# Last expert's second layer in the last chunk: one PSUM bank per output block, each block added and stored whole

## The chip, the cores and the metric

The kernel runs on 1 core of one Trainium2 chip. The metric is device microseconds of one execution. The core's engines are named as the profile names them: PE (TensorE, matmuls; PEld is its weight load), DVE (VectorE), ACT (ScalarE), POOL (GpSimd) and SP (SyncE, which only issues DMAs here). A "q" behind an engine's name (SPq, ACTq) means its instruction queue. A store is started by an issue on the queue of SP, ACT or POOL; the data is then moved by 16 DMA engines that all queues share.

## What is computed

The reference is pooled attention, and then a mixture of four experts whose weights are the tokens' normalized domain probabilities:

```python
k_p = k.reshape(B, H, Sp, pool, D).mean(axis=3); v_p = likewise      # B=8 H=8 S=576 D=64, pool 8
attn = softmax(q @ k_p^T / sqrt(D));  x = (attn @ v_p) as 4608 x 512
p = domain_probs / (domain_probs.sum(-1) + 1e-9)
for e in range(4):
    h = maximum(x @ w1[e], 0)          # 512 -> 1024
    out += p[:, e:e+1] * (h @ w2[e])   # 1024 -> 512
```

The output is 4608 x 512 in float32, 8 batches of 576 rows.

## The kernel before, in words

The work goes in nine chunks of 512 tokens. Chunks 0 to 7 are the first 512 rows of each batch; chunk 8, the last, gathers the remaining 64 rows of all eight batches. In chunk 8 a block r (0 to 3) of 128 tokens holds the 64 rows of batch 2r on partitions 0 to 63 and the 64 rows of batch 2r+1 on partitions 64 to 127. The running sum of the experts is `acc` in SBUF: 128 partitions x 4 blocks x 512 columns of float32.

The order of all instructions on every engine is written out by hand (`manual_schedule`, L1069). For each (chunk, expert) the first layer is seven block products on each of two units (`up_product`, L728 for its matmuls), and the second layer of the pair before runs between them as seven products of another kind (`down`, L796), with two PSUM banks called `chains`. The results of `down` go to `acc` in `add` (L875 on DVE, and for one step ACT's L808 and POOL's L810). With the last expert of a chunk, `down` also stores two blocks x 256 columns at a time (L885, SP's queue).

The last pair, chunk 8 and expert 3, has no first layer to run beside, so its second layer is a plain product, `down_last` (matmuls at L855). It runs after everything else on PE. The output falls into 8 pieces, 4 blocks x 2 halves of 256 columns; each piece is 8 matmuls with a free size of 256. The pieces go in the order (block 2, col 0), (3, 0), (2, 1), (3, 1), (0, 0), (1, 0), (0, 1), (1, 1). Two pieces share one PSUM bank of 512 columns, with the exception of the last two, of which the last has `chains[0]`. When both pieces of a pair are done, DVE adds them to `acc` (L875), and `store` (L890) writes the pair: one DMA for each of the two batches, 64 partitions each, on the queues of SP and ACT (for the pair of blocks 0 and 1 in column half 0, SP and POOL). The last two pieces are added and stored singly, again with one DMA per batch. In all there are 10 stores: 5 by SP, 4 by ACT and 1 by POOL.

In these stores the pattern on the DRAM side is arranged with the row as its slowest index, and this is the line that does it:

```python
by_batch = out.rearrange("(b s) d -> s b d", s=S)[NT:S]
```

The columns 256 to 511 of the first half of w2's rows come from `room`, reloaded by `load_last_weights`, as the kernel had overwritten them with weight sums.

Of the kernel before, what the change touches and what calls it, by code (L numbers as in the profile page):

```python
# [17 lines left out]
def kernel(  # L18
# [10 lines left out]
    nc = tc.nc  # L29

    B, H, S, D = q.shape
    E, DM, F = moe_w1.shape
    P = nc.NUM_PARTITIONS
# [3 lines left out]
    NT = 512  # L37
    NR = NT // P
    REM = S - NT
    KC = DM // P  # L40
    FCH = F // P
# [15 lines left out]
    HF, HN, HD, HK = FCH // 2, NT // 2, DM // 2, KC // 2  # L57
    FH = F // 2
    LO, HI = slice(0, HF), slice(HF, FCH)
    BLOCKS = 2  # L60
# [4 lines left out]
    att = psum.tile([P, 2, NT], F32, name="att")  # L65
    units = [None, None]
    chains = [psum.tile([P, NT], F32, name=f"o_ps{i}") for i in range(2)]
# [9 lines left out]
    acc = const.tile([P, NR, DM], F32, name="acc")  # L77
# [701 lines left out]
    def down(c, e, step, flip=0, pooled=()):  # L779
# [34 lines left out]
        if e == E - 1 and step in (1, 4, 5, 6):  # L814
            store(c, row, cols)
# [21 lines left out]
    def last_weights(fc, col):  # L837
        if col and fc < HF:
            return room[:, fc, :]
        return w2_bf[:, E - 1, fc, col * HD:(col + 1) * HD]  # L840

    def down_last(c, e):

        H_sb = hidden[(c, e)]
        banks = units[0] + units[1]
        for row in (1, 0):
            for col in range(2):
                cols = slice(col * HD, (col + 1) * HD)
                both = [banks[2 * row + col]] * BLOCKS
                if not row and col:  # L850
                    both[1] = chains[0]
                ps = [ps[:, j * HD:(j + 1) * HD] for j, ps in enumerate(both)]
                for j in range(BLOCKS):
                    for fc in range(FCH):
                        nc.tensor.matmul(  # L855
                            ps[j], lhsT=H_sb[:, fc // HF, row, fc % HF, j * P:(j + 1) * P],
                            rhs=last_weights(fc, col),
                            start=(fc == 0 and (j == 0 or both[1] is not both[0])),
                            stop=(fc == FCH - 1), skip_group_check=True,
                        )  # L860
                for j in range(BLOCKS):
                    add(ps[j], c, e, row * BLOCKS + j, cols, False)
                    if not row and col:
                        store(c, row, cols, j)
                if row or not col:
                    store(c, row, cols)

    def add(o_ps, c, e, r, cols, first):

        prob = p_all[:, c * NR + r, e:e + 1]  # L870
        dst = acc[:, r, cols]
        if e == 0 and first:
            nc.scalar.activation(out=dst, in_=o_ps, func=ACT.Copy, scale=prob)  # L873
        else:
            nc.vector.scalar_tensor_tensor(  # L875
                out=dst, in0=o_ps, scalar=prob, in1=dst, op0=ALU.mult, op1=ALU.add,
            )

    def store(c, row, cols, j=None):
        rs = slice(row * BLOCKS, (row + 1) * BLOCKS)  # L880
        if j is not None:
            rs = slice(rs.start + j, rs.start + j + 1)
        if c < B:
            rows = out[c * S:c * S + NT, :].rearrange("(p r) d -> p r d", r=NR)
            nc.sync.dma_start(out=rows[:, rs, cols], in_=acc[:, rs, cols])  # L885
        else:
            by_batch = out.rearrange("(b s) d -> s b d", s=S)[NT:S]
            second = nc.scalar if row or cols.start else nc.gpsimd
            for bb, queue in enumerate((nc.sync, second)):
                queue.dma_start(  # L890
                    out=by_batch[:, 2 * rs.start + bb:2 * rs.stop:2, cols],
                    in_=acc[bb * REM:(bb + 1) * REM, rs, cols],
                )

    nc.vector.memset(zeros, 0.0)

# [170 lines left out]
    with tc.manual_schedule(  # L1069
# [39 lines left out]
        for g in range(7 * N + 1):  # L1109
            t, i = divmod(g, 7)  # L1110
# [22 lines left out]
            if g == 7 * (N - 2):  # L1133
                load_last_weights()
        down_last(*order[-1])
# [1 line left out]
_INS = ['q', 'k', 'v', 'moe_domain_probs', 'moe_w1', 'moe_w2']  # L1137
# [26 lines left out]
```

## Time and profile before

| | |
|---|---|
| runs | 490.93 us median of 3 (490.93, 501.43, 489.06) |
| profiled execution's own time | 489.22 us |
| its span, first to last instruction | 487.5 us |
| granted TensorE clock | 1.000 |
| PE busy | 479.6 us (98% of the span) |
| DVE / ACT / POOL busy | 376.7 / 303.8 / 125.2 us |
| `down_last` on PE (L855) | 64 matmuls, from 476.2 us on |
| its last add on DVE | starts at 483.37 us, 0.48 us |

Times inside the execution are counted from the span's start. The profile lists busy time by engine, the chain of work that ended last, groups of instructions with their mean duration, and for DMAs the packets by queue, with the time that packets took as a share of 16 engines over the window asked for. A "packet" of a store is one contiguous run of bytes (here 1 KB, 256 columns of float32); packets of 4 bytes are listed too, among those "under 512 B". "To landing" is the time from a DMA's issue until its semaphore tells of its end.

### The profile page before, as it was taken

How to read it: one execution, taken by the hardware profiler on the slowest of the kernel's cores; microseconds unless marked ns; L12 is line 12 of the kernel's file. 1: busy time of each engine (PE TensorE's matmuls, PEld its weight loads, DVE VectorE, ACT ScalarE, POOL GpSimd, SP SyncE). 2: the span in 40 equal slices, each digit the busy share in tenths (PEclk: the TensorE clock that was granted, in tenths of full speed). 3: DMA queues.
4: the chain of work that ended last, by engine and by line, in shares of the span. 5: the costliest groups of instructions: out<-in, count | busy, mean ns of one | idle time of the engine just before them, and what ended most of it. 6: DMA issues, size and time to landing. Idle time of an engine off the chain costs nothing.

```text
span 487.5 us, 11523 instructions
## 1 busy us (share of the span) xinstructions
PE 479.6 (98%) x4667; PEld 409.1 (84%) x4672; DVE 376.7 (77%) x759; ACT 303.8 (62%) x577; POOL 125.2 (26%) x135
## 2 busy tenths in 40 slices
PE   8999999999999999999999999999999999999996
PEld 4678478898888888888889888888888888888885
DVE  5869799899768976797579866997678766876674
ACT  5778446855676567656765667656755567556650
POOL 8420504254623154016321442111011101010001
PEclk9999999999999999999999999999999999999999
DMA  9999999884897589646954396312111010004003
GB/s 198 204 207 203 206 158 172 95 98 50 107 104 59 87 79 138 41 88 54 157 49 91 28 171 60 69 23 67 34 23 23 23 65 3 12 23 87 1 2 87
DMA packets 104213, 41.97 MB, mean 86 GB/s; under 512 B 74288, under 2 KB 104112, under 8 KB 104160
## 3 DMA queue, kind: packets, MB, share of 16 engines
q0 software_dynamic: 59168, 22.54, 42.7%
q1 hardware_dynamic: 44016, 17.78, 17.3%
q10 hardware_dynamic: 976, 0.92, 0.6%
q8 instruction: 36, 0.59, 0.5%
q14 instruction: 17, 0.14, 0.1%
HBM read 45.69 MB, written 9.44 MB: 113 GB/s over the span
## 4 chain that ended last, share of the span: by engine, by line
PE 88%; DMA 8%; POOL 2%; DVE 1%; issue 0%; POOLq 0%
PE unit L728 41%; PE o_ps L796 40%; DMA wt_bf<-in_v_dram 4%; DMA w_bf<-in_moe_w_dram 3%; PE att L493 2%; PE o_ps L822 1%; PE unit L855 1%; POOL w_bf L207 1%; POOL wt_bf L142 1%; PE att L419 1%; PE unit L419 0%; DVE wt_bf L294 0%; PE att L822 0%; PE att L546 0%; PE att L529 0%
## 5 line engine op out<-in xcount | busy, mean ns | idle before, releaser
L875 DVE SCALAR_TENSOR_TENSOR acc<-o_ps,p_all,acc 128x256 f32<-128x256 f32 (+1 forms) x284 | 126.3, 485 | 50.4 <-PE o_ps L796 34.0
L796 PEld LDWEIGHTS <-H 128*128 128x128 bf16 x1320 | 129.1, 98 | 15.0
L728 PEld LDWEIGHTS <-w_bf 128*128 128x128 bf16 x1088 | 105.2, 98 | 13.0 <-issue 0.2
L708 DVE CUSTOM_DVE_ANT_0 H<-unit,partial 128x512 bf16<-128x512 f32 x128 | 87.4, 685 | 23.8 <-ACT partial L743 11.5
L796 PE MATMUL o_ps<-w_bf,H 128*128 128x256 bf16 x792 | 102.6, 272 | 0.0
L728 PE MATMUL unit<-xT,w_bf 128*128 128x256 bf16 x704 | 100.4, 273 | 0.0
L810 POOL TENSOR_TENSOR acc<-acc,addend 128x512 f32<-128x512 f32 x24 | 30.4, 1266 | 249.0 <-ACT addend L808 189.0
L743 ACT COPY partial<-unit 128x512 f32<-128x512 f32 x128 | 72.2, 591 | 30.0 <-PE unit L728 30.0
L728 PEld LDWEIGHTS <-wu_bf 128*128 128x128 bf16 x816 | 77.6, 98 | 11.7 <-issue 2.5
L728 PE MATMUL unit<-xs,wu_bf 128*128 128x256 bf16 x512 | 77.0, 273 | 0.0
L796 PE MATMUL o_ps<-wt_bf,H 128*128 128x256 bf16 x528 | 68.4, 273 | 0.0
L745 ACT ACTIVATE H<-unit 128x512 bf16<-128x512 f32 x66 | 39.9, 606 | 31.0 <-PE unit L728 30.9
L796 PEld LDWEIGHTS <-S 128*128 128x128 bf16 x528 | 51.7, 98 | 6.0
L749 ACT ACTIVATE H<-unit 128x512 bf16<-128x512 f32 x66 | 39.6, 601 | 25.6 <-PE unit L728 25.3
L741 ACT COPY unit<-unit 128x512 f32<-128x512 f32 x68 | 39.4, 582 | 23.6 <-PE unit L728 18.0
L728 PE MATMUL unit<-xs,w_bf 128*128 128x256 bf16 x256 | 38.4, 273 | 0.0
L873 ACT ACTIVATE acc<-o_ps,p_all 128x256 f32<-128x256 f32 x72 | 30.6, 484 | 9.5 <-PE o_ps L796 7.9
L152 POOL DMA_DIRECT2D kraw<-in_k_dram x20 | 26.5, 1326 | 37.0 <-DMA kraw<-in_k_dram 37.0
L728 PE MATMUL unit<-xT,wu_bf 128*128 128x256 bf16 x240 | 35.7, 272 | 0.0
L796 PE MATMUL o_ps<-wt_bf,S 128*128 128x256 bf16 x264 | 34.2, 273 | 0.0
L796 PE MATMUL o_ps<-w_bf,S 128*128 128x256 bf16 x264 | 34.2, 273 | 0.0
L152 POOL DMA_DIRECT2D vraw<-in_v_dram x20 | 29.0, 1450 | 19.5 <-DMA vraw<-in_v_dram 19.3
(171 smaller groups left out, 509.7 us busy)
## 6 DMA issues: line engine op xcount, KB each, us to landing
out_dram<-acc SPq DMA_DIRECT2D x32, 256.0 KB, 4.3
w_bf<-in_moe_w_dram POOLq DMA_DIRECT2D x12, 512.0 KB, 18.5
q_sb<-in_q_dram POOLq DMA_DIRECT2D x7, 512.0 KB, 11.1
vraw<-in_v_dram POOLq DMA_DIRECT2D x22, 144.0 KB, 6.5
kraw<-in_k_dram POOLq DMA_DIRECT2D x21, 144.0 KB, 6.0
w_bf<-in_moe_w_dram POOLq DMA_DIRECT2D x4, 256.0 KB, 7.1
w_bf<-in_moe_w_dram POOLq DMA_DIRECT2D x1, 1024.0 KB, 13.9
wt_bf<-in_k_dram POOLq DMA_DIRECT2D x4, 144.0 KB, 5.5
```

The lines of the kernel that those rows point to most:

```text
L152: nc.gpsimd.dma_start(out=raw[:], in_=rows_of(src, b, 2 * part, 2 * part + 2), accum_op=ALU.add if part else ALU.bypass)
L493: nc.tensor.matmul(c_ps[:, h // NPAIR, at:at + D + 1], lhsT=expT[:, h, r // 2, r % 2, :], rhs=vp[:, h, :], skip_group_check=True,)
L708: nc.vector._custom_dve(TENSOR_ADD_SAT, out=dst, in0=ps, in1=part, s0=LARGEST, s1=0.0)
L728: nc.tensor.matmul(ps[:, n * HN:(n + 1) * HN], lhsT=lhs[:, kc, f:f + P], rhs=rhs[:, kc, :], start=(not grows and n == 0 and kc == 0), stop ...
L741: nc.scalar.copy(out=banks[1][:], in_=ps)
L743: nc.scalar.copy(out=part[:, step - 2], in_=ps)
L745: nc.scalar.activation(out=quarter(0, 0), in_=ps, func=ACT.Relu)
L749: nc.scalar.activation(out=quarter(0, 1), in_=ps, func=ACT.Relu)
L796: nc.tensor.matmul(ps[:, j], lhsT=lhs[:, i, j * P:(j + 1) * P], rhs=rhs[:, i, :], start=(not grows and i == 0 and j == 0), stop=(i == HF - 1),
L810: nc.gpsimd.tensor_add(out=dst, in0=dst, in1=addend[:])
L873: nc.scalar.activation(out=dst, in_=o_ps, func=ACT.Copy, scale=prob)
L875: nc.vector.scalar_tensor_tensor(out=dst, in0=o_ps, scalar=prob, in1=dst, op0=ALU.mult, op1=ALU.add,)
```

## The change

`down_last` gets a PSUM bank per piece (seven banks in turn, the eighth piece takes the first again), adds each piece as soon as it is done, and stores each piece whole, 128 partitions in one DMA, by SP and ACT in turn. The last piece is stored by both queues, one batch each. The order of the pieces and of their matmuls stays. The store of the other chunks (L885) stays as it is. The pattern on the DRAM side of the new stores is arranged with the batch as its slowest index.

```diff
     def down_last(c, e):
         H_sb = hidden[(c, e)]
-        banks = units[0] + units[1]
-        for row in (1, 0):
-            for col in range(2):
-                cols = slice(col * HD, (col + 1) * HD)
-                both = [banks[2 * row + col]] * BLOCKS
-                if not row and col:
-                    both[1] = chains[0]
-                ps = [ps[:, j * HD:(j + 1) * HD] for j, ps in enumerate(both)]
-                for j in range(BLOCKS):
-                    for fc in range(FCH):
-                        nc.tensor.matmul(
-                            ps[j], lhsT=H_sb[:, fc // HF, row, fc % HF, j * P:(j + 1) * P],
-                            rhs=last_weights(fc, col),
-                            start=(fc == 0 and (j == 0 or both[1] is not both[0])),
-                            stop=(fc == FCH - 1), skip_group_check=True,
-                        )
-                for j in range(BLOCKS):
-                    add(ps[j], c, e, row * BLOCKS + j, cols, False)
-                    if not row and col:
-                        store(c, row, cols, j)
-                if row or not col:
-                    store(c, row, cols)
+        banks = [att[:, 0]] + [unit[bank][:] for bank in range(2) for unit in units] + [chain[:] for chain in chains]
+        blocks = [(r, col) for rows in ((2, 3), (0, 1)) for col in range(2) for r in rows]
+        for n, (r, col) in enumerate(blocks):
+            ps = banks[n % len(banks)][:, 0:HD]
+            cols = slice(col * HD, (col + 1) * HD)
+            for fc in range(FCH):
+                nc.tensor.matmul(
+                    ps, lhsT=H_sb[:, fc // HF, r // 2, fc % HF, (r % 2) * P:(r % 2 + 1) * P],
+                    rhs=last_weights(fc, col),
+                    start=(fc == 0), stop=(fc == FCH - 1), skip_group_check=True,
+                )
+            add(ps, c, e, r, cols, False)
+            store_block(r, cols, (nc.scalar, nc.sync) if n == len(blocks) - 1 else (nc.sync, nc.scalar)[n % 2:][:1])
...
+    def store_block(r, cols, queues):
+        by_batch = out.rearrange("(b s) d -> b s d", s=S)[:, NT:S]
+        n = 2 // len(queues)
+        for i, queue in enumerate(queues):
+            queue.dma_start(
+                out=by_batch[2 * r + i * n:2 * r + (i + 1) * n, :, cols],
+                in_=acc[i * n * REM:(i + 1) * n * REM, r, cols],
+            )
```

`store` loses its branch for the last chunk and its argument j.

More of the change, by code (lines that the diff above doesn't have):

```diff
@@ L877, in add, with store @@
             )
-    def store(c, row, cols, j=None):
+    def store(c, row, cols):
         rs = slice(row * BLOCKS, (row + 1) * BLOCKS)
[L881 to L893, printed above, removed]
+        rows = out[c * S:c * S + NT, :].rearrange("(p r) d -> p r d", r=NR)
+        nc.sync.dma_start(out=rows[:, rs, cols], in_=acc[:, rs, cols])
+    def store_block(r, cols, queues):
[6 more added lines that the diff above has]
+            )
     nc.vector.memset(zeros, 0.0)
```

## The prediction

> **What bounds the kernel now.** I read the page first (span, busy time, chain), then the timeline from 462 us on, then SP's waits, then the DMA view of the tail and of one store in a quiet stretch.
>
> ```profile
> span 487.5 us, 11523 instructions
> PE 479.6 (98%) x4667; PEld 409.1 (84%) x4672; DVE 376.7 (77%) x759; ACT 303.8 (62%) x577; POOL 125.2 (26%) x135
> PE 88%; DMA 8%; POOL 2%; DVE 1%; issue 0%; POOLq 0%
> ```
>
> PE is the bound until its last matmul. The change touches only what starts at 476.2 us, so the question is what that last stretch becomes. The timeline:
>
> ```profile
> 476.07 6.98 PEld L855 LDWEIGHTS <-H 128*128 128x128 bf16 x64
> ...
> 476.46 0.87 DVE L875 SCALAR_TENSOR_TENSOR acc<-o_ps,p_all,acc 128x256 f32<-128x256 f32 x2
> ...
> 478.18 0.88 DVE L875 SCALAR_TENSOR_TENSOR acc<-unit,p_all,acc 128x256 f32<-128x256 f32 x2 [0.86 <-PE unit L855]
> ...
> 479.09 5.58 SPq L890 DMA_DIRECT2D out_dram<-acc  x5
> 479.09 5.30 ACTq L890 DMA_DIRECT2D out_dram<-acc  x4
> ...
> 483.37 0.48 DVE L875 SCALAR_TENSOR_TENSOR acc<-o_ps,p_all,acc 128x256 f32<-128x256 f32 x1 [0.39 <-PE o_ps L855]
> ```
>
> DVE waits for PE before each pair, and the last add ends at 483.85. The last two stores are issued at 483.88, and the span ends at 487.5: 3.6 us are the last store's way and the program's end. SP's queue waits there for the stores:
>
> ```profile
> SPq L1159 <- DMA out_dram<-acc: 1.3, 2, 1.0
> ```
>
> The DMA view of 478 to 487.5 us gives all stores of the tail:
>
> ```profile
> DMA packets 1089, 1.06 MB, mean 111 GB/s; under 512 B 160, under 2 KB 1056, under 8 KB 1088
> ...
> q1 hardware_dynamic: 592, 0.52, 24.3%
> q10 hardware_dynamic: 448, 0.39, 12.7%
> q0 software_dynamic: 48, 0.13, 4.7%
> ```
>
> And the same view of 331 to 333.5 us shows one earlier store (L885, 128 partitions of two 1 KB runs) with nothing beside it; SP issues it at 331.28:
>
> ```profile
> DMA  0000000000000000002599999999997400000000
> ...
> DMA packets 272, 0.26 MB, mean 105 GB/s; under 512 B 16, under 2 KB 272, under 8 KB 272
> ...
> q1 hardware_dynamic: 272, 0.26, 30.8%
> ```
>
> Two readings carry the forecast. First, each hardware store leaves 16 small packets beside its data, however much data it has: 272 = 256 + 16 for L885; 592 = 512 + 5 x 16 for SP's five stores (q1) and 448 = 384 + 4 x 16 for ACT's four (q10). I read them as one mark for each of the 16 DMA engines that took a share. Second, the time of one 1 KB packet on one engine. Quiet: 30.8% of 16 x 2.5 us is 12.3 us, over 256 packets 48 ns. In the tail, where three queues meet: q1 24.3% of 16 x 9.5 us is 36.9 us over 512, 72 ns; q10 19.3 us over 384, 50 ns.
>
> **The change part by part.** *Matmuls.* 64 before and after, the same operands in the same order, 0.109 us apart. Cost 0 as long as no bank is late. The new banks: att's last reader in the trace is at 416.5 (L456); the four unit banks are read last by ACT's L749 at 474.20 (0.60) and DVE's L708 at 475.86 (0.68), the chains by L875 until 477.33. Piece n starts at 476.2 + 0.87 n, so the latest unit bank (piece 4, at 479.7) has 3.2 us in hand, the chains (pieces 5 and 6, at 480.5 and 481.4) 3 us and more; piece 7 takes att again, whose add ends near 477.8. PE ends as before. If a bank were late, its delay would go straight to the end.
>
> *Adds.* Eight of 0.44 to 0.48 us, as before, each now behind its own 0.87 us of matmuls; they keep up with PE. The last one waits for the last matmul in both kernels: 0. The first add moves forward by 0.87: piece 0 is done at 477.31, DVE is free at 477.33, the add ends at 477.8 and the first store is issued at about 477.83 instead of 479.09.
>
> *Issues.* 10 become 9, and POOL's goes (its landing took 3.1 us, off the path). SP issues pieces 0, 2, 4, 6 and half of 7, ACT pieces 1, 3, 5 and half of 7. One issue takes 0.50 to 0.79 us on its queue, and each queue has one in 1.75 us, so SP's for piece 6 (from 483.0) is over by 483.8, just before the last add ends. ACT has no compute after 474.8 and nothing is queued behind its issues; on SP only the program's end is. If an issue took 0.9 us instead, the last would slip 0.05. Cost 0.
>
> *The store's shape.* This is the large unknown. The pairs were written with the row as the slowest index on the DRAM side (64 rows), out of 64 partitions. A whole piece is written with the batch as the slowest index: 2 batches x 64 rows, out of 128 partitions. No store in the trace has a slowest count other than 64 or 128, so its spread over the engines must be bounded. *Lower end:* it goes over 16 engines like all others, 128 packets in 8 x 48 ns = 0.4 us; pieces come every 0.87 us and no queue builds. It may even gain: the last stores landed 2.5 to 2.9 us after issue, the quiet one (by the same view) after 2.1. So -0.6 to 0. *Upper end:* the engines get equal whole slices of the slowest index, as the count of 16 allows in every store shown (4 of 64 rows or 8 of 128 each). Then the only slices that both sides share are two, and 14 of 16 engines stand idle: 64 packets on each of two engines for every piece, 64 x 48 ns = 3.1 us, with a new one each 0.87 us, on the same two engines whichever queue issued it.
>
> I take the upper end: all the stores shown are explained by one cut along the slowest index, and reaching 16 engines from 2 x 64 rows would need a second cut, for which I see no row. The last piece, by two stores of 64 rows each, would still go over 16 engines, but its packets on those two wait behind the rest.
>
> The Trainium skill (DMA: Bandwidth & Descriptors, section "Why a DMA increments its semaphore by 16 and not by 1") states that the engine count is the largest number up to 16 that divides both patterns' slowest counts above 1; by it the pieces have 2 engines and the sum is the one below, where the 16 engines of every store shown would leave it at or a little under the time before. No run here yet shows a store with a small slowest count. The same page ("Rules for kernel authors") speaks for the change in advising one 128-partition transfer over two halves; the trace's 48 ns against 50 and 72 fits that, and by it alone the sum would be some tenths of a us lower.
>
> *The sum.* First issue 477.83; first packet 1.4 later (the tail's first data stands at 480.5 for an issue at 479.09; the quiet store took 0.85): 479.2. Seven pieces x 64 packets, and 2 x 4 of the last stores, are 456 packets on each of the two engines, x 48 ns = 21.9: data ends at 501.1. From the last data to the span's end is 1.4 before (486.1 to 487.5): 502.5. Around the span lie 489.22 - 487.5 = 1.72: **504.2 us**, 15.0 or 3.1% above the profiled execution before. That one lies below the median shown (490.93); on the median the same step gives 505.9. I took 48 ns since the new stores, like the quiet one, have 128 partitions, and since no more than two engines ask for anything. With the 72 ns of the crowded tail the packets take 32.8 and the time is 515.1; with the quicker first packet (0.85) it is 503.7.
>
> **The rivals.** *All 16 engines, not slower.* For it: every store shown. Against it: none of those has the new shape. Then the tail is issued at 483.88 as before, with less ahead of it: 488.6 to 489.3, about 489.0. The point from which this decides: k engines take 128/k x 48 ns for a piece, and keep up with 0.87 us if k is 8 or 16. *Four engines,* if the cut goes one level deeper: 7 x 32 + 8 = 232 packets, 11.1 us, 493.4, still within 2%. *Two engines at the crowded price:* 515.1; for it the 72 ns of q1, against it that 16 engines worked then. *A PE wait for a bank* in place of the pair's shared bank: the 3 us in hand speak against it; a whole missed add costs 0.5 us, 489.7.
>
> **How the numbers follow.** Two engines 0.76 (of this 48 ns likelier than 72), 16 engines 0.19 with the bank wait in it, four or eight 0.05. The likeliest case's own range is 503 to 515. As it holds under 0.8, the range must reach the 16-engine case: 488.6 to 515.1. 2%, about what a measurement of this kernel can tell from no change, is 499.0 on the profiled time and 500.7 on the median; all of the two-engine case lies above both but for a small part: slower 0.75. The rest is within 2%: 0.24. Faster by 2% would need 10 us out of a tail of 3.6: 0.01.
>
> **What would show it.** In the profile after: PE's last matmul and DVE's last add near 483.4 and 483.9 as before (matmul and add steps); first store issued near 477.8; in the tail's DMA view, under 512 B, 2 small packets for each whole store and 16 for each of the last two (7 x 2 + 2 x 16 = 46) if two engines work, 9 x 16 = 144 if all do; a mean DMA share near 2/16 until about 501 us, at some 43 GB/s (2 x 1 KB in 48 ns). A landing that grows from store to store, and an end that waits for it on SP. Wrong would be: 144 small packets and a span near 487; a PE gap at L855; or two engines with a packet well off 48 ns.

## The result, and the profile after

| | before | changed kernel |
|---|---|---|
| median of 6 runs each | 489.07 us (488.51 to 501.43) | 502.50 us (502.01 to 505.64) |
| ratio to before | | 1.0281, 95% interval 1.025 to 1.0312 |
| span of the profiled execution | 487.5 us | 503.9 us |

The change made the kernel slower by 13.4 us (the prediction: 15.0, to 504.2). The ratios in this document leave out executions well above the others of their kernel: the 501.43 us here, and 509.4 us (granted clock 0.942) of the version with four whole stores further below, whose time is given without it. The page after:

```profile
span 503.9 us, 11527 instructions
PE 481.9 (96%) x4672; PEld 410.1 (81%) x4672; DVE 376.7 (75%) x759; ACT 303.7 (60%) x577; POOL 124.7 (25%) x134
PE 93%; ACT 1%; DMA 1%; POOL 1%; issue 0%; DVE 0%; POOLq 0%
```

The span grew by 16.4 us, and PE is busy no more than 2.3 us longer. Three of the 16.4 belong to this one execution and lie far from the change: the granted clock fell between 15 and 20 us, where it was 1.00 before, and all that follows comes 3.0 us later. The other executions of the changed kernel have spans of 500.3 to 501.9 us. The window table of the changed kernel (length, busy time by engine, then PEclk, DMA share, GB/s) has it in its third column from the right:

```profile
15.00:20.00 5.00, 4.61 (x33) 3.65 (x32) 2.05 (x5) 2.04 (x4) 2.75 (x4) 0.50 1.38 204
```

The tail, from the timeline after. Take 3.0 us off each time to lay it beside the one before:

```profile
480.25 0.48 DVE L866 SCALAR_TENSOR_TENSOR acc<-att,p_all,acc 128x256 f32<-128x256 f32 x1
480.76 13.96 SPq L880 DMA_DIRECT2D out_dram<-acc  x5
...
481.69 11.48 ACTq L880 DMA_DIRECT2D out_dram<-acc  x4
...
486.36 0.48 DVE L866 SCALAR_TENSOR_TENSOR acc<-att,p_all,acc 128x256 f32<-128x256 f32 x1 [0.39 <-PE att L851]
```

PE and DVE do what they did: the last add starts at 486.36 - 3.0 = 483.36 (483.37 before), and the first store is issued at 480.76 - 3.0 = 477.8 (479.09 before). But the issues of the two queues stretch over 14.0 and 11.5 us instead of 5.6 and 5.3, and the program's end comes 17 us after the last add instead of 3.6. At the end SP waits for stores, for longer than the 1.3 us of before:

```profile
SPq L1147 <- DMA out_dram<-acc: 7.7, 4, 3.7
```

The DMA view of 470 to 504 us shows why:

```profile
DMA  0000000000000011111111111111423111111100
GB/s 0 0 0 0 19 0 0 0 0 10 0 0 0 0 30 42 29 48 43 45 48 36 48 48 48 48 48 48 116 67 96 48 48 48 48 48 48 48 16 0
DMA packets 1073, 1.08 MB, mean 32 GB/s; under 512 B 46, under 2 KB 1070, under 8 KB 1070
...
q1 hardware_dynamic: 600, 0.59, 5.5%
q10 hardware_dynamic: 470, 0.46, 4.3%
```

A share of one tenth of 16 engines over 20 us, a plateau of 48 GB/s, and 46 small packets. 46 is 7 x 2 + 2 x 16: two engines for each whole store, 16 for each of the last two, which are the short rise between 494 and 496 us.

### The profile page after: what moved, and what is told of

It is laid out like the page before. It is cut to its first block, busy times and chain, and to the rows that moved or that the text cites. A ratio compares the mean times of both kernels' runs of the same rounds, so it can differ in the third digit from the quotient of the medians.

```text
span 503.9 us, 11527 instructions
## 1 busy us (share of the span) xinstructions
PE 481.9 (96%) x4672; PEld 410.1 (81%) x4672; DVE 376.7 (75%) x759; ACT 303.7 (60%) x577; POOL 124.7 (25%) x134
## 4 chain that ended last, share of the span: by engine, by line
PE 93%; ACT 1%; DMA 1%; POOL 1%; issue 0%; DVE 0%; POOLq 0%
PE unit L728 41%; PE o_ps L796 40%; PE o_ps L822 2%; PE att L493 1%; DMA wt_bf<-in_v_dram 1%; PE o_ps L650 1%; PE att L419 1%; POOL wt_bf L142 1%; PE unit L851 1%; PE unit L650 1%; PE o_ps L664 1%; PE unit L419 1%; PE att L664 1%; ACT qT L404 0%; PE att L851 0%; PE o_ps L851 0%
```

## The experiments

The theory under test: a store's engines are set by the slowest count that both sides share (the runs vary it on the DRAM side alone; the SBUF side has 64 or 128 partitions throughout); seven stores with a slowest count of 2 run on two DMA engines, which then have 456 packets of 1 KB each to move. The rivals: the bank per block and the early adds cost the time; a whole block in one DMA blocks its queue, whatever its pattern; only a store near the end costs. Ratios below are to the kernel before on the same chip, with their 95% intervals.

**Each half of the change alone.** First the stores alone, in the kernel before (`store_block` is that of the change):

```diff
+                single = not row and col    # the last two blocks
                 for j in range(BLOCKS):
                     add(ps[j], c, e, row * BLOCKS + j, cols, False)
-                    if not row and col:
-                        store(c, row, cols, j)
-                if row or not col:
-                    store(c, row, cols)
+                    if single:
+                        store_block(row * BLOCKS + j, cols, (nc.scalar, nc.sync) if j else (nc.sync,))
+                if not single:
+                    for j in range(BLOCKS):
+                        store_block(row * BLOCKS + j, cols, ((nc.sync, nc.scalar)[j],))
```

> The kernel before with its shared banks and its paired adds kept; only its stores are replaced by the change's: each block whole, batch slowest on the DRAM side, SP and ACT in turn, the last block by both queues. Theory (two slices of the slowest DRAM index, so two DMA engines carry the seven whole stores): the whole loss, and as the first store is issued about 1.3 us later than with single adds, slightly more: 503 to 504.5 us against about 489 before, 46 small packets. Rival (the loss comes from the bank per block and the early adds): about 489. Rival (a queue that blocks in its issue whatever the pattern): also about 503, so this run does not tell that one apart.

Measured: 504.1 us, ratio 1.0296 (1.0272 to 1.032), 46 small packets. The stores are the whole loss. The time is 1.6 us above the changed kernel's 502.5, as a first store made late by adds in pairs would give, but the two ratios' intervals overlap, so these 1.6 us are not shown.

Then banks and adds alone, in the changed kernel (`store` is that of the kernel before):

```diff
             add(ps, c, e, r, cols, False)
-            store_block(r, cols, ...)
+            row, j = divmod(r, BLOCKS)
+            if not row and col:
+                store(c, row, cols, j)
+            elif j:
+                store(c, row, cols)
```

> The changed kernel's bank per block and single adds, with the stores of the kernel before (pairs, one DMA per batch, row slowest). Theory: no loss, 488.5 to 489.5 us, first store near 479.1 as before, under 512 B 160 packets. Rival (banks and early adds cost the time): about 502. If the bank per block gains something, it is at most 0.5 us.

Measured: 488.44 us, ratio 0.9977 (0.9964 to 0.999), 160 small packets. The rival of the banks is out.

**The same store with another order of indices.** The seven whole stores keep their size, packets, queues and times; what changes is which DRAM index is slowest, and with it the row that each packet goes to:

```diff
+        if len(queues) == 1:
+            by_row = out.rearrange("(b s) d -> s b d", s=S)[NT:S]
+            queues[0].dma_start(out=by_row[:, 2 * r:2 * r + 2, cols], in_=acc[:, r, cols])
+            return
...
```

> The changed kernel with one thing different: the seven whole stores are written with the row as the slowest DRAM index and the batch inside it. Same 128 KB, same 128 one-KB packets, same queue and order, one DMA each. The rows of the last chunk come out permuted in these seven blocks (partition p goes to batch p mod 2, row p div 2), so the output is not the reference's. Theory: all 16 engines again, 144 small packets (9 x 16), 488 to 489.5 us. Rival (a whole store of 128 partitions blocks its queue, or one DMA per block is too much for one queue): 500 us or more, with issues of several us as in the changed kernel.

Measured: 488.57 us, ratio 0.9977 (0.9962 to 0.9992). Its DMA view of 478 to 489.5 us:

```profile
DMA packets 1169, 1.06 MB, mean 92 GB/s; under 512 B 144, under 2 KB 1168, under 8 KB 1168
...
out_dram<-acc SPq DMA_DIRECT2D x4, 128.0 KB, 2.1
out_dram<-acc ACTq DMA_DIRECT2D x3, 128.0 KB, 2.1
```

144 is 9 x 16, and a whole store lands in 2.1 us. A whole block by one queue is no burden that shows; the order of the DRAM indices is worth the 13.9 us between this run and the changed kernel.

**Every block by one DMA per batch,** as the change does with its last:

```diff
-            store_block(r, cols, (nc.scalar, nc.sync) if n == len(blocks) - 1 else (nc.sync, nc.scalar)[n % 2:][:1])
+            store_block(r, cols, (nc.scalar, nc.sync) if n % 2 else (nc.sync, nc.scalar))
```

> The changed kernel with every block stored by both queues, one batch each (64 rows, 64 partitions), as the change does with its last block alone: 16 stores instead of 9. Theory: 16 engines each, 256 small packets, 488 to 489.5 us; against the kernel before possibly 0.3 to 0.8 us less, since the stores start 1.3 us earlier and POOL's store is gone from the tail. Rival (single adds or many issues cost): 490 or more; each queue then has one issue of 0.5 to 0.8 us in 0.87 us, so a late last issue would show at 484 or later on the timeline of before.

Measured: 488.49 us, ratio 0.9981 (0.9965 to 0.9996), 256 small packets. 16 issues cost nothing that shows. Unlike the run with the row slowest, this version puts every row in its place, so it is the repair that a kernel can use.

**Other counts.** With 4 and with 8 as the slowest count, the rows of a batch walked as 4 x 16 and 8 x 8, by batch on both queues:

```diff
...
+            dst = by_batch[2 * r + i, :, cols]
+            if n > 1:    # 4, or 8; 1 for the last block
+                dst = dst.rearrange("(t h) d -> h t d", h=n)
+            queue.dma_start(out=dst, in_=acc[i * REM:(i + 1) * REM, r, cols])
```

> The changed kernel with seven blocks stored by one DMA per batch on both queues, and on the DRAM side 64 rows walked as 4 x 16 (slowest index 4: row 4t + h, h slowest), so the rows inside each batch come out permuted and the output is not the reference's there; the last block as in the change. Theory (the slowest count sets the number of engines): 4 engines, 14 stores x 16 + 8 = 232 packets on each, 224 fewer than in the changed kernel, x 45 ns = 10.1 us less: about 492.4, between 491.5 and 493.5, 14 x 4 + 2 x 16 = 88 small packets. Rival (only a batch as slowest index, or only 2, does it; otherwise a second cut spreads it over 16): 488 to 489.5.

> As the kernel with four slices, with 8 x 8 rows instead (slowest index 8; rows inside a batch permuted, last block as in the change). Theory: 8 engines, 14 x 8 + 8 = 120 packets on each, 5.4 us of work in the 7 us between first and last store, so no backlog: 488 to 489.5 us, 14 x 8 + 2 x 16 = 144 small packets. This is the point at which the prediction said that the engines keep up. Rival (any small slowest count costs in proportion): 490 or more.

Measured: 493.76 us with four (ratio 1.0095, 1.0065 to 1.0125), 489.15 us with eight (ratio 1.0008, 0.9989 to 1.0026). The DMA views, first of the kernel with four over 476 to 491.7 us:

```profile
GB/s 0 0 0 0 0 5 42 86 73 97 81 65 50 50 63 37 55 81 78 97 89 97 86 76 83 97 99 99 120 164 162 180 102 94 94 84 10 0 0 0
DMA packets 1113, 1.06 MB, mean 67 GB/s; under 512 B 88, under 2 KB 1112, under 8 KB 1112
```

and of the kernel with eight over 476 to 487.3 us:

```profile
DMA packets 1169, 1.06 MB, mean 94 GB/s; under 512 B 144, under 2 KB 1168, under 8 KB 1168
```

Both counts of small packets are as expected (14 x 4 + 2 x 16 = 88; 14 x 8 + 2 x 16 = 144), and four engines level off at 97 GB/s, twice the 48 of two. So the count itself sets the engines. The run with four lies 0.3 us above its range: from the thirteenth to the seventeenth slice it moves 37 to 63 GB/s, so the four engines were not kept full. In that kernel SP waited 3.5 us in three pieces for earlier stores before it could issue; the runs with four whole stores, next, go into that.

**The dose.** The first four blocks whole, the last four by batch:

```diff
+            both = (nc.scalar, nc.sync) if n % 2 else (nc.sync, nc.scalar)
+            store_block(r, cols, both[:1] if n < 4 else both)
```

> The changed kernel with its first four blocks stored whole (by SP and ACT in turn) and the last four by one DMA per batch on both queues. Theory (two engines have a backlog of 64 packets for each whole store): 4 x 64 + 4 x 8 = 288 packets on each of the two engines instead of 456; the changed kernel's trace has 456 in 20.6 us, 45 ns each, so 7.6 us less than its 502.5: about 494.9, between 494 and 496. Rival (only a whole store near the end costs, as its landing is waited for): about 489.

Measured: 496.68 us, ratio 1.0147 (1.0121 to 1.0172): the backlog is there and the rival out, but 1.8 us more than the sum of packets (497.1 and 2.2 in the next expectation count the 509.4 us in). The trace is of the execution of 509.4 us. Its matmuls run at a clock of 0.95, but its tail is like the others': 16.9 us from the first store's issue to the end, where their spans of 494.6 to 495.8 us leave 16.8 to 18.0 if the first issue stands at 477.8. The wait in it that the sum did not have is SP's own, ahead of two of its issues (total, times, longest):

```profile
SPq L881 <- DMA out_dram<-acc: 8.1, 2, 4.8
```

In the trace the ends of SP's and ACT's stores are told by eight semaphores in turn, so a ninth store is not issued until the one eight before has ended; here the last store of all shares its semaphore with the fourth whole one, is issued when that ends, at 504.55, and the span ends 3.1 us later. The test keeps the packets and lessens the stores, blocks 0 and 1 in column half 0 as a pair:

```diff
-            store_block(r, cols, both[:1] if n < 4 else both)
+            if n in (4, 5):
+                if n == 5:
+                    store_pair(cols)    # one DMA per batch, two blocks
+            else:
+                store_block(r, cols, both[:1] if n < 4 else both)
```

> Four whole stores as in the run with four (which came out at 497.1, not at the 494.9 expected); then blocks 0 and 1 in column half 0 as a pair, one DMA per batch (row slowest), and only the last two blocks singly: 10 stores instead of 12. The same 288 packets of 1 KB on each of the two engines. Theory for the missing 2.2 us: in that run's trace SP's last store waited to be issued until an earlier whole store had ended (waits of SP on stores 8.1 us in two; every ninth store shares its semaphore with one eight before); with 10 stores the last two share with the first two, which end early, so the wait goes: 494 to 495.5. Rival (four whole stores simply cost more per packet on the two engines): 496.5 to 497.5 again.

Measured: 495.13 us, ratio 1.0123 (1.0105 to 1.0141), in the theory's range. It is 1.5 us below the version with 12 stores, but the two ratios' intervals overlap, so the cost of the wait is not settled. Nor did the wait go as I wrote; there is one left:

```profile
SPq L890 <- DMA out_dram<-acc: 4.2, 1, 4.2
```

It is shorter in sum, and the last stores now move their data before the two engines have emptied their backlog, so nothing stands behind it. In the DMA view of 476 to 493.1 us, SP's last one is the 93 and 132 GB/s, ahead of the last stretch of 48:

```profile
GB/s 0 0 0 0 0 5 34 38 43 34 24 48 48 48 48 48 43 53 89 117 117 113 144 209 177 180 194 65 48 93 132 53 48 48 48 48 38 0 0 0
```

A single whole store, the seventh, with all others by batch:

```diff
+            store_block(r, cols, both[:1] if n == 6 else both)
```

> The changed kernel with only the seventh block stored whole, by SP; all others by one DMA per batch on both queues. Theory: its 64 packets on each of two engines begin 1.3 us after an issue at about 482.97 and take 45 to 62 ns each (the changed kernel's first store had 62 ns while alone), 2.9 to 4.0 us, so data ends at 487.2 to 488.3, and the run at 490.3 to 491.4; the version with all blocks by batch measured 488.49. Rival (only a backlog of several costs anything): within 0.3 us of 488.5.

Measured: 491.02 us, ratio 1.0042 (1.0029 to 1.0055), 2.5 us above the version with all blocks by batch, and in the range of the theory. One such store near the end is enough to set it.

**What limits the two engines: queue, packets or bytes.** All whole stores by SP:

> The changed kernel with all seven whole stores issued by SP; the last block still by both queues. Theory (two DMA engines are the bound, and both queues feed the same two): no change, 502 to 504 us. Rival (each queue's issue, which took up to 5.4 us in the changed kernel, limits the rate): SP alone would be slower; with the 62 ns per packet that SP's first store had alone, 448 packets take 27.8 us instead of 20.6: about 510.

The edit is `(nc.sync,)` in place of the turn. Measured: 502.26 us, ratio 1.0259 (1.0235 to 1.0283), as with two queues. The queue is not the limit. Then blocks 2 and 3 in packets of 2 KB:

```diff
+            if r >= BLOCKS:
+                if col:
+                    store_block(r, slice(0, DM), ((nc.sync, nc.scalar)[n % 2],))
+            else:
                 store_block(r, cols, ...)
```

> The changed kernel with blocks 2 and 3 stored with both column halves at once, in packets of 2 KB (2 batches x 64 rows x 512 columns), after their second half; blocks 0 and 1 as in the change. The first store starts 1.75 us later. If a packet costs by its bytes (2 KB in about 90 ns): the same work, 1.75 us later: about 504.2. If it costs a fixed 45 ns: 128 packets fewer on each engine, 5.8 us less: about 498.5. The theory (two engines) holds in either case; this sizes its term.

Measured: 503.99 us, ratio 1.03 (1.0273 to 1.0328): bytes, as longer packets won nothing. Two engines move 48 GB/s, 24 each.

**A version that beats both?** Banks and adds of the change, stores of before, POOL's store given to ACT (`second = nc.scalar`):

> Bank per block and single adds, stores as in the kernel before, with POOL's one store given to ACT. A candidate that beats both: the version with POOL's store measured 488.44. If POOL's long packets delay the last stores (they stand among them in the tail of the kernel before), 0.2 to 0.5 us less: about 488.1; if they do not, the same within 0.3 us.

Measured: 488.55 us, ratio 1.0001 (0.9986 to 1.0016). POOL's long packets cost nothing that shows. The version by batch and the one with banks alone are 0.2% faster than before by their own comparisons, with intervals that end just below 1; this one, which differs from the second by a single store, is the same as before. So the bank per block with 16-engine stores is worth 0 to 0.2%, and which of the two is not settled.

## Why the prediction was right, by its own steps

*Matmuls and adds, cost 0:* right. No PE gap at L851, the last add at the same place, and the run with banks and adds alone within 0.6 us of before. The PE wait for a bank did not come.

*First store 1.26 us earlier:* right (477.8 on the timeline of before). What it was worth under the loss is not settled: with the adds in pairs the time was 1.6 us greater, with intervals that overlap.

*Issues, cost 0:* the cost held, the durations did not. An issue was put at 0.50 to 0.79 us; in the changed kernel they took up to 5.4, and SP's last one began at 489.64 - 3.0 = 486.6 instead of 483.88. It cost nothing because the backlog of the two engines lasted 13 us longer still.

*The store's shape, two engines:* right, and it is the whole result. The choice between the bounds had no row to stand on, only the reading that one small packet marks one engine and that one cut along the slowest index explains all stores. The runs have now borne that out: slowest counts of 2, 4, 8 and 64 gave 2, 4, 8 and 16 small packets for each store, and the same bytes in another order took the loss away. The Trainium skill (DMA: Bandwidth & Descriptors, section "Why a DMA increments its semaphore by 16 and not by 1") has this as the largest number up to 16 that divides both slowest counts above 1; the runs agree, with 46, 88 and 144 small packets. The advice of the Trainium skill that was weighed there too (the same page, "Rules for kernel authors"), one 128-partition transfer over two halves, stood the wrong way for this pattern: two halves by batch took 488.5 us, one whole with the batch slowest 502.5, and one whole with the row slowest 488.6. The 48 ns against 50 and 72 were no evidence for it: the 50 and the 72 are both of stores in halves.

*The sum:* 1.4 us to the first packet was 1.3; 456 packets took 20.6 us (482.0 to 502.6) instead of 21.9, 45 ns each instead of 48 (why a little quicker, no run shows); and 1.3 instead of 1.4 from the last data to the end. That is 1.5 us less than predicted, which with a before 0.15 us lower gives 502.5 for 504.2. The crowded price of 72 ns held for no more than the first 2 us, 57 packets at 70 ns each.

*The rival with 16 engines,* 489.0, is what the reordered pattern measured (488.57); *the one with four,* 493.4, was met by the run with a slowest count of 4 (493.76); and eight engines keep up, as the point of decision said.

*Not seen ahead:* a store that waits for the semaphore of the store eight before. In the changed kernel, with nine stores, it did not show, in the run with four whole stores it may be the 1.8 us that the sum of packets left open.

## What to carry to other kernels

Look at the slowest index of a store's DRAM side before its size: a whole block in one transfer lands in 2.1 us with 64 rows slowest, and is 3 us of work for two engines with 2 batches slowest. The small packets in the DMA view tell how many engines a store got, so one count over a window settles the question. And the sum for a tail is the bytes on each busy engine, not the bytes over 16: at 1 KB in 45 ns, eight engines hid everything here and four did not.

## What the runs showed of the hardware that I had not expected

*An issue can block its queue.* With two engines behind, an issue on SP or ACT no longer takes half a microsecond. The changed kernel, by line and queue (min/median/max in ns):

```profile
L880 SPq DMA_DIRECT2D out_dram<-acc x5: 512/679/5077, 480.8 to 489.6; - x5
L880 ACTq DMA_DIRECT2D out_dram<-acc x4: 522/1890/5355, 481.7 to 487.8; - x4
```

With all whole stores on SP, its median issue took 2.5 us, about the time that the two engines need for one such store. Nothing stood behind these issues here; that compute behind them on ACT's queue would wait too is likely, but no run shows it.

*The second queue did not share from the start.* ACT's first store was issued at 481.69, but until 485.5 only SP's packets (q1) moved. The DMA view of 482 to 485.5 us of the changed kernel:

```profile
DMA packets 125, 0.14 MB, mean 39 GB/s; under 512 B 0, under 2 KB 124, under 8 KB 124
...
q1 hardware_dynamic: 124, 0.13, 13.0%
```

These are SP's first store nearly whole (128 packets, 64 on each of two engines), so ACT's first began when that was done. From 487 us on, both queues move the same number of packets (138 each from 487 to 493). In the stretch shown the first 57 packets took 2 us, and the 67 after 484 only 1.5 us. The second queue is not what made the start slow: with all whole stores on SP, the first 2 us moved 60. Why ACT's store waited, and what the slow start is, no run shows.

*The granted clock falls some time after PE's end.* In the changed kernel PE ends at 486.3 us, the clock reads 0.99 from 488 to 489 and 0.50 from 489 on; in the kernel before, whose span ends 4 us after its PE, it stays at 1.00. A window in the middle of the tail of the changed kernel:

```profile
496.00:502.00 6.00, 0.00 (x0) 0.00 (x0) 0.00 (x0) 0.00 (x0) 0.00 (x0) 0.50 0.14 48
```

The mean clock of about 0.985 in the executions with a long tail is that idle stretch (15 us at 0.50 in 501) and cost nothing. The dip at 15 to 20 us did cost time: there PE was busy for 4.61 of 5 us. What set it off, no run shows.
